# Retention and a squared-ReLU FFN: four heads in each half of x, a first stretch written out by hand

## The chip, the cores and the metric

The kernel runs on one core of one Trainium2 chip. The metric is the device time of one execution in microseconds (us); lower is better. The engines that matter are PE (TensorE, the matrix unit), DVE (VectorE), ACT (ScalarE), POOL (GpSimd) and SP (SyncE, which here only issues transfers). Each engine works through its own queue in order.

## The reference

The inputs q, k and v are float32 arrays of (8 batches, 8 heads, 576 positions, 64); w_in (512 x 2048) and w_out (2048 x 512) are float64 and are turned into float32 on the chip. Cut to what matters:

```python
scores = scale * np.matmul(q, k.transpose(0, 1, 3, 2))
gamma = 1.0 - 2.0 ** (-5.0 - np.arange(H))
Dmat = np.where(rel >= 0, gamma[:, None, None] ** rel, 0.0)   # rel = row - column
ret = scores * Dmat
attn = np.matmul(ret, v)
x = attn.transpose(0, 2, 1, 3).reshape(B * S, H * D)          # 4608 x 512
h = np.maximum(x @ w_in, 0.0)
out = h * h @ w_out
```

## The kernel before

**Two phases.** Phase one computes the retention (attn) chunk by chunk and feeds it into the first FFN product, g = relu(x @ w_in)², which goes to DRAM. Phase two (from about 565 us) reads g back and multiplies it by w_out. Both FFN products use a scheme with 7 products of sub-blocks in place of 8 (PRODUCTS), so sums of blocks are made by DVE; only the first block of 512 tokens is done plainly (`first_in`).

**Chunks.** The 576 positions of a batch are four chunks of 128 and one of 64; there are 40 chunks (`chunks`). A state matrix u (64 x 64 per head) carries what came before, so a chunk is two halves of 64 rows. For chunk i:

- `load(i)` transfers q, k and v from DRAM. q and k use three transfers each (L148 and L150, one half of the heads and then two groups of swapped heads), v one (L145).
- `scale_q(i)` multiplies q by its decay (L375: DVE for chunk 0, POOL for others); `scale_v(i)` does it for v (L468, POOL).
- `turn(i)` transposes k and q on PE into one PSUM tile of two banks (L422), one bank for each half of the rows. ACT copies all of k out of both banks (L425), DVE all of q (L426).
- `scores(i)` multiplies them on PE (L449), and DVE masks the result (L459 for chunks 0 to 3, L461 later).
- `retain_a` makes the second half's own products (L480) and adds the first half to u (L483); ACT copies u out (L489). `retain_b` multiplies q by u (L515). `retain_c` makes the first half's own products (L566) and adds the second half to u (L560). `x_out` lets ACT copy the result into xT (L543). The tiles x_ps and u_ps have one buffer each.

From chunk 11 on, DVE transposes by blocks (`flip`, L396), ACT moves the blocks (L411), and `whole` takes the place of the retain functions.

**Heads and halves of x.** xT holds x with its columns over 128 partitions and four groups. Before, group hp held the heads 2hp and 2hp+1 in its two halves of the partitions, as w_in lies in DRAM, so one transfer brought a piece of w_in. For hp of 2 and 3 the heads of q and k are swapped within a pair (`HEADS`, the third entry b is the half), so that the matmuls reach all four quarters of the array in turn; the two groups of swapped heads in `load` come from this.

**w_in.** It comes in 16 pieces of 512 KB (`fetch_w`, L196). Each piece is turned from 64-bit words into float32 in six parts (`round_parts`): one and two (L210, L214, DVE), beside (L218, L219, ACT), three, four and five (L222, L225, L228, DVE). `convert(n)` issues the next n parts. `fetch_raw(n)` issues the next n pieces, up to six ahead of the pieces that are done.

**The first block.** `first_in(j, halves)` multiplies piece j with xT (L671) for half of the 512 tokens (four matmuls of 256 columns) or all of them (512 columns), ACT applies Relu (L676), and DVE squares (L679). Half pieces 0 to 2 run as soon as the first 256 tokens are there.

**The order of the first stretch** is a loop with conditions on i (L856 to L898): for chunk i the retain functions of chunk i-1, then scores(i), scale_q(i+1) and turn(i+1), with convert and first_in between them and fills of idle matmuls (`warm`, L836 and L839).

**Pace.** After chunk 4, `ffn(i, half)` issues as many FFN steps as PACE asks for at the number of tokens that have gone by: pairs of (tokens, steps), with straight lines between. A block n of later FFN steps (`ffn_in`, L707) starts with four sums of x (`sum_x`, L633 to L636). They are issued one by one in the last steps of the block before, if block n's x is complete by then, and otherwise in a row at its start.

Of the kernel before, what the change touches and what calls it, by code (L numbers as in the profile page):

```python
# [40 lines left out]
def kernel(  # L41
# [90 lines left out]
    def load(i, names="qkv"):  # L132
# [4 lines left out]
        for name, pool, src in (("q", ld3, q), ("k", ld5, k), ("v", ld4, v)):  # L137
            if name not in names:
                continue
            t = got["qkv".index(name)] = pool.tile([128, H, D], F32, tag=name, name=f"{name}_ld")  # L140

            issue = nc.scalar if i == 0 and name != "q" else nc.sync
            at = src[b, :, c0:c0 + cs, :].rearrange("h s d -> s h d")
            if name == "v":
                issue.dma_start(t[:cs], at)  # L145
            else:

                issue.dma_start(t[:cs, 0:H // 2, :], at[:, 0:H // 2, :])  # L148
                for e in range(2):
                    issue.dma_start(t[:cs, H // 2 + e::2, :], at[:, H // 2 + 1 - e::2, :])  # L150
# [22 lines left out]

    def piece_src(j):
        wi, m, e = pieces[j]
        f = (m + e * N_M) * 128
        if wi == 0:
            return moe_w_in.rearrange("(c p) f -> p c f", p=128)[:, :, f:f + 128]
        return moe_w_out[f:f + 128, :].rearrange("p (c f) -> p c f", c=N_DM)

# [13 lines left out]
    def fetch_w(j):  # L194
        if j < len(pieces) and wide:
            nc.sync.dma_start(raw_of(j).bitcast(I64).rearrange("p (c f) -> p c f", c=N_DM), piece_src(j))  # L196
# [4 lines left out]
    def round_parts(j):  # L201
# [28 lines left out]
        if not wide:  # L230
            to = t if pieces[j][0] == 0 else t.rearrange("p o s f -> p (o s) f")
            return [lambda: nc.sync.dma_start(to, piece_src(j))] + [lambda: None] * 5
# [96 lines left out]
    load(1)  # L329
    fetch_raw(1)  # L330
    load(2)

# [22 lines left out]
    HEADS = [(hp, e, e if hp < HP // 2 else 1 - e) for hp in range(HP) for e in range(2)]  # L355

    def rows(half, n=64):
        return slice(64 * half, 64 * half + n)

# [52 lines left out]
    def turn(i):  # L414
# [10 lines left out]
        nc.scalar.copy(to[:, 1].rearrange("p d h t -> p h d t"), p[:, :n_h, 1, :, :])  # L425
        nc.vector.tensor_copy(to[:, 0].rearrange("p d h t -> p h d t"), p[:, :n_h, 0, :, :])  # L426
# [44 lines left out]
    def x_at(hp, b, h):  # L471
        return xp[0][rows(b), hp // 2, 0:256].rearrange("p (g t) -> p g t", g=2)[:, hp % 2, CH * h:CH * h + CH]

    def within(i, h):

        s = st[i]
        b_, ci, c0, cs = chunks[i]
        own, grow = [], []
        for hp, e, b in HEADS:
            own.append(lambda hp=hp, e=e, b=b: nc.tensor.matmul(  # L480
                x_at(hp, b, h), lhsT=s["vs"][rows(h), 2 * hp + b, :], rhs=s["ret"][rows(h), e, hp, :],
                start=clears(b, hp // 2), stop=False, skip_group_check=True))
            grow.append(lambda hp=hp, e=e, b=b: nc.tensor.matmul(  # L483
                u_ps[0][rows(e), hp, :], lhsT=loaded[i][1][rows(1 - h), 2 * hp + e, :], rhs=s["vs"][rows(1 - h), 2 * hp + b, :],
                start=(ci == 0 and h == 1 and hp == 0), stop=(hp == HP - 1), skip_group_check=True))
        return own, grow
# [4 lines left out]
    def retain_a(i):  # L491
# [4 lines left out]
        if ci == 0:  # L496
            u_ps[0] = ps_u.tile([128, HP, D], F32, tag="u", name="u_ps")
        if cs < C:
            return
        own, grow = within(i, 1)  # L500
        for j in range(0, len(own), 2):
            for f in own[j:j + 2] + grow[j:j + 2]:
                f()
        grown(i, 0)

    def retain_b(i):
# [3 lines left out]
        for h in reversed(range(cs // CH)):  # L510
# [3 lines left out]
            for hp, e, b in HEADS[0:2] + HEADS[4:6] + HEADS[2:4] + HEADS[6:8]:  # L514
                s["read"] = nc.tensor.matmul(  # L515
                    x_at(hp, b, h), lhsT=u[rows(e), hp, :], rhs=s["qT"][rows(e), hp, CH * h:CH * h + CH],
                    start=clears(b, hp // 2), stop=False, skip_group_check=True)
# [11 lines left out]
    def x_out(i, after):  # L529
# [5 lines left out]
        while at < tok + cs:  # L535
# [7 lines left out]
            nc.scalar.copy(xT[n][:, :, at - n * TOK:end - n * TOK].rearrange("p (a g) t -> p a g t", a=2),  # L543
# [10 lines left out]
    def grow_of(i, h):  # L554

        ci = chunks[i][1]
        if ci == 0 and h == 0:
# [3 lines left out]
            u[rows(e), hp, :], lhsT=loaded[i][1][rows(h), 2 * hp + e, :], rhs=st[i]["vs"][rows(h), 2 * hp + b, :],  # L561
            start=(ci == 0 and h == 0 and hp == 0), stop=(hp == HP - 1), skip_group_check=True) for hp, e, b in HEADS]

    def own_of(i, h, first):
        s = st[i]
        return [lambda hp=hp, e=e, b=b: nc.tensor.matmul(  # L566
            x_at(hp, b, h), lhsT=s["vs"][rows(h), 2 * hp + b, :], rhs=s["ret"][rows(h), e, hp, :],
            start=clears(b, hp // 2), stop=False, skip_group_check=True)
            for e in (first, 1 - first) for hp, e_, b in (HEADS[j] for j in (e, e + 4, e + 2, e + 6))]

# [10 lines left out]
    def whole(i):  # L581
# [16 lines left out]
        for h in range(cs // CH):  # L598
# [3 lines left out]
            for hp, e, b in HEADS[0:2] + HEADS[4:6] + HEADS[2:4] + HEADS[6:8]:  # L602
                m = nc.tensor.matmul(x_at(hp, b, h), lhsT=u[rows(e), hp, :], rhs=s["qT"][rows(e), hp, CH * h:CH * h + CH],
                                     start=clears(b, hp // 2), stop=False, skip_group_check=True)
# [168 lines left out]
    def step():  # L773
# [11 lines left out]
    PACE = ((4 * TOK + HALF // 4, N_0 + 2 * N_MP * NP - 2), (5 * TOK - HALF, N_0 + 3 * N_MP * NP - 2),  # L785
            (6 * TOK + HALF // 4, N_0 + 4 * N_MP * NP - 2), (8 * TOK + HALF // 4, N_0 + 6 * N_MP * NP - 2),
# [45 lines left out]
    def warm(count, wide):  # L832
        t = ps_f.tile([128, 512], F32, tag="f", name="idle_ps")
        for _ in range(count):
            if wide:
                nc.tensor.matmul(t[:, 0:128], lhsT=idle, rhs=idle, start=True, stop=True)  # L836
            else:
                for b in range(2):
                    nc.tensor.matmul(t[rows(b), 0:64], lhsT=idle[rows(0), rows(b)], rhs=idle[rows(0), 0:64], start=True, stop=True,  # L839
# [353 lines left out]
```

## Time and profile before

Five executions took 967.4 to 969.11 us, with a median of 967.99. The profiled execution:

| | |
|---|---|
| its own time | 969.06 us |
| span, from the first to the last instruction | 967.3 us |
| mean granted PE clock | 0.993 |
| copy of chunk 0's x, of chunk 1's (L543 starts) | 15.40 us, 24.69 us |
| copy of chunk 2's x, of chunk 3's (L543 starts) | 33.16 us, 38.68 us |
| first half piece of the FFN (L671) | 25.42 us |
| first piece over 512 tokens (L671, 512 columns) | 49.13 us |
| issues of q: of 128 KB, of 64 KB, of 32 KB | 32, 72, 16 (those of the short chunks among them) |
| v, 256 KB: median from issue to landing | 4.1 us |
| w_in piece, 512 KB: median from issue to landing | 5.8 us |

A row of the timeline has its start, its length, the engine, the line of the kernel, the operation, what it writes and reads, and in brackets how long the engine had been idle before it and what ended that. Times are from the start of the span. A matmul of float32 shows as two records.

### The profile page before, as it was taken

To read this page: it belongs to the slowest core of one execution; us is meant where nothing else is said; L and a number is where in the kernel's file an instruction comes from. 1 tells how busy PE (TensorE), PEld (TensorE's weight loads), DVE (VectorE), ACT (ScalarE), POOL (GpSimd) and SP (SyncE) were. 2 spreads that over 40 slices of the span, in tenths; PEclk is the share of its full clock that TensorE was granted. 3 is DMA by queue.
4 is the path that set the end of the run, shared out by engine and by line. 5 is a ranking of instruction groups with operands and counts; after the bars stand their busy time and mean duration, and the time that the engine had idled before them with its cause. 6 is when DMAs were issued, how large, how long until landed. Compare 5 with 4: busy or idle time off the path is not lost. (4 is left out here: it accounts for less than half of the span.)

```text
span 967.3 us, 24021 instructions
## 1 busy us (share of the span) xinstructions
PE 949.4 (98%) x10108; PEld 855.1 (88%) x10108; DVE 781.0 (81%) x1447; ACT 337.3 (35%) x808; POOL 129.8 (13%) x121
## 2 busy tenths in 40 slices
PE   6999999999999999999999999999999999999998
PEld 6755788888878888888888899999999999999998
DVE  3789799988897877988966597887888787887876
ACT  2544375865655866657621000000000000000000
POOL 3221223212213123222110000000000000000000
PEclk8999999999999999999999999999999999999999
DMA  9885657576649666684177966445354454524241
GB/s 204 224 226 152 184 164 198 172 248 201 192 133 289 185 159 198 201 244 143 61 293 292 357 247 255 155 157 186 123 194 163 160 197 162 203 99 174 88 175 44
DMA packets 172012, 181.43 MB, mean 188 GB/s; under 512 B 118144, under 2 KB 132480, under 8 KB 165248
## 3 DMA queue, kind: packets, MB, share of 16 engines
q1 hardware_dynamic: 169792, 179.38, 58.3%
q8 instruction: 79, 1.29, 0.6%
q10 hardware_dynamic: 2112, 0.52, 0.3%
q14 instruction: 29, 0.24, 0.1%
HBM read 109.36 MB, written 70.52 MB: 186 GB/s over the span
## 5 line engine op out<-in xcount | busy, mean ns | idle before, releaser
L707 PE MATMUL h_b<-room,w 128*128 128x256 f32 x768 | 183.4, 382 | 2.6 <-DVE room L634 1.9
L411 ACT COPY qk<-flip 32x256 f32<-32x256 f32 x416 | 167.4, 402 | 8.4 <-DVE flip L396 2.3
L707 PEld LDWEIGHTS h_b<-room,w 128*128 128x128 f32 x768 | 144.3, 190 | 24.1 <-issue 2.2
L1042 PE MATMUL o_b<-w,room 128*128 128x128 f32 x1168 | 144.4, 275 | 0.2 <-DVE room L994 0.2
L1042 PEld LDWEIGHTS o_b<-w,room 128*128 128x128 f32 x1168 | 137.2, 192 | 0.4 <-DVE room L994 0.4
L1042 PE MATMUL o_c<-w,room 128*128 128x128 f32 x1008 | 123.0, 275 | 0.0
L707 PE MATMUL h_a<-room,w 128*128 128x256 f32 x512 | 122.0, 381 | 0.0
L707 PE MATMUL h_c<-room,w 128*128 128x256 f32 x512 | 121.8, 381 | 0.0
L1042 PEld LDWEIGHTS o_c<-w,room 128*128 128x128 f32 x1008 | 117.7, 192 | 0.0
L707 PEld LDWEIGHTS h_a<-room,w 128*128 128x128 f32 x512 | 96.5, 190 | 14.1 <-issue 0.5
L1056 ACT COPY r<-o_a 128x128 f32<-128x128 f32 x53 | 14.1, 266 | 271.6 <-PE o_a L1042 230.9
L707 PEld LDWEIGHTS h_c<-room,w 128*128 128x128 f32 x512 | 96.6, 190 | 13.4
L1042 PE MATMUL o_a<-w,a 128*128 128x128 f32 x688 | 85.7, 275 | 0.0
L724 POOL TENSOR_TENSOR room<-room 128x512 f32<-128x512 f32 x32 | 35.8, 1119 | 342.1 <-ACT room L723 331.7
L1042 PEld LDWEIGHTS o_a<-w,a 128*128 128x128 f32 x688 | 81.2, 192 | 0.1
L714 DVE SCALAR_TENSOR_TENSOR room<-room 128x512 f32<-128x512 f32 x96 | 71.8, 748 | 3.3
L671 PE MATMUL h_ps<-room,w 128*128 128x512 f32 (+1 forms) x152 | 60.3, 545 | 1.1 <-ACT room L543 0.7
L375 POOL TENSOR_TENSOR q_ld<-q_ld,dv 128x512 f32<-128x512 f32 (+1 forms) x39 | 44.3, 1135 | 81.9 <-DMA q_ld<-in_q_dram 74.1
L468 POOL TENSOR_TENSOR v_ld<-v_ld,dv 128x512 f32<-128x512 f32 (+1 forms) x40 | 50.7, 1269 | 11.9 <-DMA v_ld<-in_v_dram 7.0
L726 DVE TENSOR_TENSOR room<-h_b,room 128x512 f32<-128x512 f32 x32 | 22.0, 689 | 37.3 <-PE h_b L707 37.3
L671 PEld LDWEIGHTS h_ps<-room,w 128*128 128x128 f32 x152 | 28.6, 196 | 24.2 <-issue 20.6
L566 PE MATMUL x_ps<-qk,v_ld 64*64 64x64 f32 x1024 | 49.6, 224 | 0.0
(109 smaller groups left out, 1381.4 us busy)
## 6 DMA issues: line engine op xcount, KB each, us to landing
g_dram<-room SPq DMA_DIRECT2D x32, 1280.0 KB, 5.7
a<-g_dram SPq DMA_DIRECT2D x30, 1024.0 KB, 6.0
room<-g_dram SPq DMA_DIRECT2D x15, 1024.0 KB, 5.7
w<-w_dram SPq DMA_DIRECT2D x7, 1792.0 KB, 9.7
out_dram<-room SPq DMA_DIRECT2D x17, 512.0 KB, 3.3
w<-in_moe_w_in_dram SPq DMA_DIRECT2D x16, 512.0 KB, 5.8
w<-in_moe_w_out_dram SPq DMA_DIRECT2D x16, 512.0 KB, 4.4
v_ld<-in_v_dram SPq DMA_DIRECT2D x31, 256.0 KB, 4.1
```

The costliest lines, as they stand in the source:

```text
L375: engine.tensor_tensor(t, t, dv[:cs, :, NCH + ci:NCH + ci + 1].to_broadcast([cs, H, D]), op=ALU.mult)
L411: nc.scalar.copy(*moves.pop(0)[2:])
L468: nc.gpsimd.tensor_tensor(vs[:cs], vs[:cs], dv[:cs, :, ci:ci + 1].to_broadcast([cs, H, D]), op=ALU.mult)
L566: return [lambda hp=hp, e=e, b=b: nc.tensor.matmul(x_at(hp, b, h), lhsT=s["vs"][rows(h), 2 * hp + b, :], rhs=s["ret"][rows(h), e, hp, :], ...
L671: nc.tensor.matmul(p.rearrange("p h t -> p (h t)"), lhsT=w[:, c, :], rhs=xT[0][:, c, lo * HT:hi * HT], start=(c == 0), stop=(c == N_DM - 1))
L707: nc.tensor.matmul(p[:, mm, :], lhsT=w[:, c, :], rhs=xs[n][right][:, c, :], start=(j in OPENS and mm == 0 and c == 0), stop=(j in CLOSES a ...
L714: nc.vector.scalar_tensor_tensor(t, t, 0.0, t, op0=ALU.max, op1=ALU.mult)
L724: nc.gpsimd.tensor_tensor(g["A11"], g["A11"], g["A11"], op=ALU.mult)
L726: nc.vector.tensor_tensor(g["A22"], p, p15, op=ALU.add)
L1042: nc.tensor.matmul(p, lhsT=s["lefts"][left][:, m, :], rhs=w_out[j][:, m, WO_SLOT[right], :], start=(i in OPENS and m == 0), stop=(i in CLO ...
L1056: nc.scalar.copy(r[:, 0, 0:128], p)
```

## The change

A half of the partitions of x now holds four heads: heads 0 to 3 in the lower, 4 to 7 in the upper (`HEADS`: b is hp // 2, and the bank of x_ps is e). q, k and the decays keep the natural order of the heads, so q and k are one transfer each. A w_in piece is now two transfers, one for each half of the partitions (`in_parts`). In `turn`, for chunks of 128, ACT copies the first bank (k and q of the first 64 rows) and DVE the second. The first stretch is written out as a list. It holds scores(1) ahead of retain_b(0), fewer idle matmuls (one pair of 512 columns in place of 28 pairs of 64), w_in pieces fetched earlier, and 29 parts of conversion by its end where there were 32. One point of PACE is gone. `within` is gone, and `retain_a` uses `own_of` and `grow_of`.

```diff
@@ load
-            at = src[b, :, c0:c0 + cs, :].rearrange("h s d -> s h d")
-            if name == "v":
-                issue.dma_start(t[:cs], at)
-            else:
-                issue.dma_start(t[:cs, 0:H // 2, :], at[:, 0:H // 2, :])
-                for e in range(2):
-                    issue.dma_start(t[:cs, H // 2 + e::2, :], at[:, H // 2 + 1 - e::2, :])
+            issue.dma_start(t[:cs], src[b, :, c0:c0 + cs, :].rearrange("h s d -> s h d"))
@@ pieces of w_in
+    def in_parts(j):
+        wi, m, e = pieces[j]
+        f = (m + e * N_M) * 128
+        for half in range(2):
+            of = slice(half * d_model // 2, (half + 1) * d_model // 2)
+            yield rows(half), moe_w_in[of, f:f + 128].rearrange("(c p) f -> p c f", p=D)
...
     def fetch_w(j):
-        if j < len(pieces) and wide:
-            nc.sync.dma_start(raw_of(j).bitcast(I64).rearrange("p (c f) -> p c f", c=N_DM), piece_src(j))
+        if j >= len(pieces) or not wide:
+            return
+        to = raw_of(j).bitcast(I64)
+        if pieces[j][0]:
+            nc.sync.dma_start(to.rearrange("p (c f) -> p c f", c=N_DM), piece_src(j))
+        else:
+            for at, part in in_parts(j):
+                nc.sync.dma_start(to[at].rearrange("p (c f) -> p c f", c=N_DM), part)
@@ start
     load(0)
-    load(1)
+    load(1, "qk")
     fetch_raw(1)
+    load(1, "v")
     load(2)
+    fetch_raw(2)
@@ heads
-    HEADS = [(hp, e, e if hp < HP // 2 else 1 - e) for hp in range(HP) for e in range(2)]
+    HEADS = [(hp, e, hp // (HP // 2)) for hp in range(HP) for e in range(2)]
...
-    def x_at(hp, b, h):
-        return xp[0][rows(b), hp // 2, 0:256].rearrange("p (g t) -> p g t", g=2)[:, hp % 2, CH * h:CH * h + CH]
+    def x_at(hp, e, b, h):
+        return xp[0][rows(b), e, 0:256].rearrange("p (g t) -> p g t", g=2)[:, hp % 2, CH * h:CH * h + CH]
@@ turn
-        nc.scalar.copy(to[:, 1].rearrange("p d h t -> p h d t"), p[:, :n_h, 1, :, :])
-        nc.vector.tensor_copy(to[:, 0].rearrange("p d h t -> p h d t"), p[:, :n_h, 0, :, :])
+        if n_h == 2:
+            nc.scalar.copy(to[:, :, :, 0, :], p[:, 0, :, :, :])
+            nc.vector.tensor_copy(to[:, :, :, 1, :], p[:, 1, :, :, :])
+        else:
+            nc.scalar.copy(to[:, 1].rearrange("p d h t -> p h d t"), p[:, :n_h, 1, :, :])
+            nc.vector.tensor_copy(to[:, 0].rearrange("p d h t -> p h d t"), p[:, :n_h, 0, :, :])
@@ retain_a
-        own, grow = within(i, 1)
-        for j in range(0, len(own), 2):
-            for f in own[j:j + 2] + grow[j:j + 2]:
-                f()
+        beside_each(own_of(i, 1, 1), grow_of(i, 0), range(0, H, 2))
         grown(i, 0)
@@ x_out
-            nc.scalar.copy(xT[n][...].rearrange("p (a g) t -> p a g t", a=2),
+            nc.scalar.copy(xT[n][...].rearrange("p (g a) t -> p a g t", a=2),
                            p[:, :, :, at - tok:end - tok])
@@ pace
-    PACE = ((4 * TOK + HALF // 4, N_0 + 2 * N_MP * NP - 2), (5 * TOK - HALF, N_0 + 3 * N_MP * NP - 2),
-            (6 * TOK + HALF // 4, N_0 + 4 * N_MP * NP - 2), (8 * TOK + HALF // 4, N_0 + 6 * N_MP * NP - 2),
+    PACE = ((4 * TOK + HALF // 4, N_0 + 2 * N_MP * NP - 2), (6 * TOK + HALF // 4, N_0 + 4 * N_MP * NP - 2), (8 * TOK + HALF // 4, N_0 + 6 * N_MP * NP - 2),
             (9 * TOK, N_0 + 7 * N_MP * NP - 2))
@@ warm
-                    nc.tensor.matmul(t[rows(b), 0:64], lhsT=idle[rows(0), rows(b)], rhs=idle[rows(0), 0:64], start=True, stop=True,
-                                     skip_group_check=True)
+                    nc.tensor.matmul(t[rows(b), :], lhsT=idle[rows(0), rows(b)], rhs=idle[rows(0), 0:1].to_broadcast([64, 512]),
+                                     start=True, stop=True, skip_group_check=True)
@@ the first stretch: the part of the loop for i <= N_EARLY goes, and this comes (two calls to a line here)
     turn(0)
+    load(3); scores(0)
+    scale_q(1, nc.gpsimd); warm(1, False)
+    turn(1); fetch_raw(1)
+    retain_a(0); convert(3)
+    scores(1); scale_q(2, nc.gpsimd)
+    retain_b(0); retain_c(0)
+    load(4); fetch_raw(2)
+    convert(2); retain_a(1)
+    turn(2); convert(1)
+    retain_b(1); retain_c(1)
+    load(5); fetch_raw(1)
+    convert(3); first_in(0, (0,))
+    convert(1); scores(2)
+    scale_q(3, nc.gpsimd); retain_a(2)
+    convert(2); turn(3)
+    first_in(1, (0,)); convert(3)
+    retain_b(2); retain_c(2)
+    load(6); fetch_raw(1)
+    convert(1); scores(3)
+    convert(2); scale_q(4, nc.gpsimd)
+    first_in(2, (0,)); convert(3)
+    retain_a(3); turn(4)
+    retain_b(3); retain_c(3)
+    load(7); fetch_raw(2)
+    step(); scores(4)
+    convert(3); scale_q(5, nc.gpsimd)
+    step(); convert(5)
+    for i in range(N_EARLY + 1, N_CH + 1):
...
@@ decays
-    order = [h if h < H // 2 else h ^ 1 for h in range(H)]
-    by_s = (gamma[order, None, None] ** s / math.sqrt(D)).transpose(2, 0, 1)
+    by_s = (gamma[:, None, None] ** s / math.sqrt(D)).transpose(2, 0, 1)
```

The other calls of x_at, `own_of` and `grow_of` follow the new indices (the bank e, and head 2hp + e in place of 2hp + b).

## The prediction

> **What bounds the kernel now.** I read the page first: span and share of each engine, then the 40 slices.
>
> ```profile
> span 967.3 us, 24021 instructions
> PE 949.4 (98%) x10108; PEld 855.1 (88%) x10108; DVE 781.0 (81%) x1447; ACT 337.3 (35%) x808; POOL 129.8 (13%) x121
> ...
> PE   6999999999999999999999999999999999999998
> ...
> DVE  3789799988897877988966597887888787887876
> ...
> PEclk8999999999999999999999999999999999999999
> DMA  9885657576649666684177966445354454524241
> ```
>
> PE is busy 98% of the span. Only the first slice (24 us) is poor, so a change can pay only by letting PE reach its full stream sooner, or by removing a hole later. The busy times by stretch show where:
>
> ```profile
> 10.00:20.00 10.00, 8.92 (x277) 8.14 (x274) 4.03 (x10) 4.08 (x8) 3.18 (x3) 0.77 1.01 252
> 20.00:30.00 10.00, 7.78 (x156) 6.66 (x155) 5.79 (x10) 2.97 (x6) 4.22 (x4) 0.66 0.59 134
> 30.00:40.00 10.00, 8.88 (x223) 7.45 (x220) 9.62 (x17) 6.00 (x14) 2.33 (x3) 1.00 0.81 196
> 285.00:290.00 5.00, 3.13 (x15) 2.47 (x14) 4.93 (x9) 3.32 (x8) 0.00 (x0) 1.00 0.01 3
> ```
>
> The columns are PE, PEld, DVE, ACT, POOL, granted clock, DMA share, GB/s. From 10 to 20 us the transfers are full (1.01) and the clock is low (0.77); from 285 to 290 us PE works 3.13 of 5. Then the timeline of PE, for what ends each gap:
>
> ```profile
> 8.42 1.13 PE L449 MATMUL sc_ps<-qk 64*64 64x64 f32 x32 [1.41 <-DVE qk L426]
> ...
> 22.22 0.80 PE L515 MATMUL x_ps<-qk,u_sb 64*64 64x64 f32 x18 [2.83 <-issue]
> ...
> 25.42 3.34 PE L671 MATMUL h_ps<-room,w 128*128 128x256 f32 x8
> ...
> 29.96 1.99 PE L671 MATMUL h_ps<-room,w 128*128 128x256 f32 x8
> ...
> 48.04 0.69 PE L449 MATMUL sc_ps<-qk 64*64 64x64 f32 x32 [1.24 <-DVE qk L426]
> 49.13 6.28 PE L671 MATMUL h_ps<-room,w 128*128 128x512 f32 x14
> ...
> 287.57 1.97 PE L707 MATMUL h_b<-room,w 128*128 128x256 f32 x8 [1.87 <-DVE room L634]
> ```
>
> The same half piece takes 3.34 us at 25.42 and 1.99 at 29.96: the clock. From 49.13 on PE runs full pieces, and the list of waits has nothing over 0.7 us on PE after that but the 1.87 at 287.57. The chain of waits goes back only to 565 us and is all PE there, so the second phase is not touched. **So I compare two times: when the first full-width piece (j=3) starts, and the hole at 287.** What PE gains there lasts to the end if DVE keeps up: in the timeline the last conversion step (L228) of pieces 5 to 15 ends 5.0 to 7.1 us before PE starts that piece.
>
> **The change, part by part.**
>
> *One transfer for q and k.* Each chunk issues 3 transfers where there were 7, 160 fewer in all. On SP an issue takes 0.46 to 0.6 us. Bytes and 256-byte runs stay, and SP sets nothing after 60 us, so later this is worth 0: PE hides it, with q scaled a chunk ahead of its use. At the start it counts: q0's last issue ended at 2.73, now it ends near 1.75. q0 came at 5.80 (DVE's scaling starts there). Between 0 (the bytes decide) and 1.0 earlier I take 0.7, as the last landing follows its issue by 3 us.
>
> *Two transfers per w_in piece.* 16 issues more, 0.6 us each on SP, 9.6 us over 100 us in which SP also drops about 48 issues: 0. The Trainium skill, page "DMA: Bandwidth & Descriptors", section "Rules for kernel authors", speaks against this: two transfers to halves of the partitions share the same engines, one over 128 partitions is better. By that rule it is 0.6 us of issue per piece for nothing, and on the path at most once, for piece 0. The split is needed here only because a half of x now holds four whole heads.
>
> *Copies by banks.* ACT's copy of k ran 7.06 to 7.65, DVE's of q from 7.68 to 8.37, one after the other on the same two banks. By banks both start at 7.06 and the longer ends at 7.75: 0.62 gained for chunk 0. For chunks 1 to 3 it lies in the chain below; from chunk 5 on PE has pieces to do meanwhile: 0.
>
> *The new order.* Scores of the first chunk start at 8.42 - 0.7 - 0.62 = 7.1. Then PE's queue as it will stand, with rows of before (low clock until 14 us, as then): scores(0) 1.13, to 8.2; the one wide idle pair, four records of 512 columns (0.43 apart at full clock, so 0.9 if side by side and up to 3.4 at half clock in a row; I take 1.7, twice the lower), to 9.9; turn(1) 1.12, 11.0; retain_a(0) 1.13, 12.1; scores(1) 1.13, 13.2; retain_b and c(0) 1.45, 14.7; the x copy and u copy 0.86, 15.5 (x_ps and u_ps have one buffer); retain_a(1) 0.7, turn(2) 0.7, retain_b and c(1) 1.46: the x of chunk 1 starts at **18.5**, before it was 24.69. The transfers allow it: by the landings of before (q1 8.15, v1 10.26, q2 13.97, v2 17.0, less 0.7), piece 0 is there at about 10.5, piece 1 at 18, q3 at 21.
>
> *Code.* Of the 24.69, 2.83 us are the wait named issue at 22.22, 0.45 another at 15.91. The page shows an instruction queue (q8, 79 packets, 1.29 MB: 16 KB each, and 1.29 MB over 20216 PE records is 64 B, so 256 records or 128 matmuls a packet). The two waits are 142 matmuls and 6.3 us apart. I read them as code that comes late while transfers are full. The change drops 104 of the 112 idle records of L839. At the new places matmul 77 is in turn(1) at 10.8, 219 at the end of retain_a(1) at 16.3, 361 in retain_a(2) after 23: 5.5 us where 6.3 were needed, then enough. So 0.8 (bounds 0 and 2.8): x of chunk 1 at 19.3.
>
> *From there to the full pieces* the order puts DVE behind PE and ACT. Each step waits for the one before: x copy 0.59, first_in(0) 1.99, scores(2) 0.65, mask 0.76, parts four and five of piece 1 1.4, first_in(1) 1.99, its Relu and the two ACT parts of piece 2 1.7, part three 0.69, mask(3) 0.76, four and five 1.4, first_in(2) 1.99, Relu and ACT parts 1.7, u copy 0.38, retain_b and c(3) 1.46: 17.5, so the x of chunk 3 at 36.8; it was 38.68. Of a lead of 5.4 only 1.9 is left: piece 2's and 3's ACT parts stand behind a Relu that waits for PE, and DVE is idle behind them. Then x copy 0.59, first_in(0) 2.0, scores(4) 0.4, mask 0.7, DVE's three to five of piece 3 2.07 (they are queued behind that mask now), a square and four shorter parts 1.9, copy 0.69, scores(5) and retain_c(4) 1.3: 9.6. Piece 3 starts at 46.4 instead of 49.13: **2.7 us gained** (0.7 with the whole code wait, 3.5 with none).
>
> Three DVE parts (2.07 us) come later than before in the count of parts by then (29, not 32). They come out of the slack of 5.0, so 0; without it PE would wait up to 2.
>
> *PACE.* The dropped point asked for 98 steps at token 2496, two short of block 4, just ahead of the chunk that completes block 4's x. So L634's sums were made in a row at the block's start. On the straight line from 70 (2064) to 126 (3088), 2496 asks for 93.6: the last steps of block 3 come after that x, and the sums go in one by one as at the other blocks. **1.87 gained**; bounds 2.24 (PEld's gap) and 0.
>
> *Head order.* x's bank now follows e. Record counts stay. Reads now alternate as scores do (x32 in 0.65 against 0.69 for reads): 0.
>
> **Sum.** 2.7 + 1.87 = 4.6. The profiled execution took 969.06 (span 967.3 and 1.76 around it): 964.5. It is 1.07 above the median 967.99, so on the median 963.4.
>
> **The clock.** The clock rose to 1.00 by 30 us with 112 small idle records, most of which go. PE's gaps in my chain stay below 2 us where before one of 2.83 stood ahead of the slow piece, so I keep the clock of before up to 14 us and full from there. The Trainium skill, "TensorE: Matmul & The Clock Gate", "Part 1: The HAM clock gate", says that the throttled state is the default and some 3.4 us of activity lift it; by it, thinner warming could hold the half clock for one window more, 1.35 on a half piece.
>
> **Rivals.**
> 1. *A longer lead*: the chain from 19.3 is less strict than I wrote it and most of the 6.2 us lasts. For: DVE works only 5.79 of 10 us from 20 to 30. Against: its order is fixed. 967.99 - 6.2 - 1.87 = 959.9.
> 2. *The start gives nothing*: code, late transfers (1.5 MB more of w_in stand ahead of chunk 5's q) or DVE take it back, and only the hole at 287 goes: 966.1.
> 3. *Slower, by the clock*: with 104 idle records gone the gate falls back at the first gap and PE runs at half rate up to the full pieces. Six half pieces at +1.35, of which one was already paid, 6.75; chunks 2 and 3 at +2.1 (scores 1.13 for 0.65, turn 1.12 for 0.71, retain in proportion): 4.2. Together 11, and 11 - 4.6 = 6.4 slower, or 2.2 if only the pieces are on the path: 970 to 974, 971 taken. It decides if the clock from 20 to 40 us is under 0.7. For: 0.66 from 20 to 30 before. Against: real work fills that stretch now.
> 4. *The copies don't run side by side*, if DVE is still busy when a bank is ready: 0.6 per chunk at most, inside the range of the forecast.
>
> **Chances.** Forecast (with rival 4) 0.57; longer lead 0.14; only the hole 0.17; slower 0.12. A measurement of this kernel tells 0.2% (1.9 us) from no change. The forecast's own range is 962 to 965.5, so it and the longer lead are faster; the third lies on the edge at 966.1, a third of it faster: 0.57 + 0.14 + 0.05 = 0.76, same 0.13, slower 0.11. The range takes in the longer lead and the third case: 959.5 to 968.3.
>
> **What would show it.** In the changed profile: scores(0) near 7.1, the two copies of a turn at the same time; the x of chunk 1 near 19 and of chunk 3 near 37; the first 128x512 piece near 46.4; no wait of h_b on L634; issue waits of PE under 1 us; clock 1.00 from 20 us. A first full piece later than 49, or holes on L707 behind conversion steps, would make me wrong; one before 43 means that I made the chain too strict.

## The result and the profile after

The changed kernel takes 969.74 us (median of 21 runs, 967.82 to 973.06), the kernel before on the same chips 967.65 (40 runs). The ratio is 1.0021, with a 95% interval of 1.0013 to 1.0029: slower by 0.2%, where 963.4, faster by 0.5%, was forecast.

The profiled execution took 973.06 us, 3.3 above the median and the slowest of the 21. Most of this excess is not at its start: from ACT's copy of x at 357.31 us to the end it needs 613.99 us, where the same stretch takes 611.6 in the profiles of e3, e4 and e17 below. First its page: the span, the slices of the span, and the queue that carries the transfers.

```profile
span 971.3 us, 23541 instructions
...
PE   7899999999999999999999999999999999999998
...
DVE  4499789988889887987976597888888788787876
...
PEclk9699999999999999999999999999999999999999
DMA  9997576686857876766168966545354454524241
...
q1 hardware_dynamic: 167520, 179.37, 61.4%
```

PE's first slice is better than before (7 for 6), the second slice now has the low clock (6). The queue is busy for 61.4% of the time, before for 58.3%, with as many bytes. Then the same stretches as before and one more; the columns are PE, PEld, DVE, ACT, POOL, granted clock, DMA share, GB/s.

```profile
10.00:20.00 10.00, 8.74 (x244) 6.74 (x240) 5.63 (x11) 4.44 (x9) 3.17 (x3) 1.00 1.24 219
20.00:30.00 10.00, 8.22 (x119) 6.19 (x123) 6.99 (x12) 3.60 (x9) 2.65 (x3) 0.83 1.11 189
30.00:40.00 10.00, 7.20 (x138) 5.67 (x132) 3.87 (x8) 3.63 (x8) 3.13 (x3) 0.67 1.13 209
40.00:50.00 10.00, 9.33 (x114) 7.34 (x114) 4.07 (x6) 2.00 (x5) 2.11 (x2) 0.65 1.13 197
285.00:290.00 5.00, 5.00 (x104) 4.28 (x103) 4.97 (x6) 1.28 (x4) 3.31 (x3) 1.00 0.23 91
```

The hole at 287 is gone: PE is busy for all 5 us. The clock column has 1.00 up to 20 us and then 0.83, 0.67 and 0.65. The 1.00 of the first 16 us can't be right; these rows of PE show it:

```profile
11.23 0.69 PE L430 MATMUL t_ps<-w,k_ld 64*128 64x64 f32 x8
...
17.71 0.47 PE L430 MATMUL t_ps<-w,k_ld 64*128 64x64 f32 x8
```

The same eight records take 0.69 us at 11.23 and 0.47 at 17.71. Before they took 0.69 at 10.76, where the column has 0.50, and 0.46 at 17.11, where it has 1.00. So PE ran at the low rate up to about 16 us, as before and some 2 us longer; the column missed it. From 21 us on the times of the half pieces agree with the column. The DMA share is higher than before (1.24 against 1.01 from 10 to 20 us) for fewer bytes (219 GB/s against 252). DVE works 3.87 of 10 us from 30 to 40, where it worked 9.62: it waits. What it waits for shows in the timelines of PE, DVE and ACT, taken together here around the second and third half piece.

```profile
20.52 1.97 PE L664 MATMUL h_ps<-room,w 128*128 128x256 f32 x8 [0.92 <-ACT u_sb L487]
26.13 3.35 PE L664 MATMUL h_ps<-room,w 128*128 128x256 f32 x8 [0.18 <-DVE w L238]
...
34.16 3.75 PE L664 MATMUL h_ps<-room,w 128*128 128x256 f32 x8 [2.80 <-DVE w L238]
...
55.23 4.99 PE L664 MATMUL h_ps<-room,w 128*128 128x512 f32 x11
```
```profile
31.12 0.69 DVE L232 SCALAR_TENSOR_TENSOR w<-w,w 128x512 f32<-128x512 uint32 x1 [2.14 <-ACT w L229]
...
40.46 0.42 DVE L438 COPY qk<-t_ps 128x256 f32<-128x256 f32 x1 [5.44 <-ACT qk L437]
```
```profile
29.52 0.38 ACT L669 ACTIVATE room<-h_ps 128x256 f32<-128x256 f32 x1 [2.94 <-PE h_ps L664]
29.80 0.71 ACT L228 ACTIVATE w<-w,exp_bias 128x512 uint32<-128x512 uint32 x1
30.41 0.68 ACT L229 ACTIVATE w<-w 128x512 f32<-128x512 uint32 x1
```

Read from the bottom up: ACT idles 2.94 us until PE has finished the half piece of 26.13, takes its Relu (L669), and only then makes its two parts of piece 2. DVE idles 2.14 us for these parts, and PE waits 2.80 us for DVE. It is a ring: each engine waits for the one before, and at half clock the PE part of it is 3.35 us where at full clock it is 1.97. The first full-width piece starts at 55.23, 6.1 later than before. From there to the end it is 971.3 - 55.23 = 916.1, where it was 967.3 - 49.13 = 918.2: 2.1 gained, although this run loses 2.7 against before behind 357.31. So the loss that a usual run has lies in the first 55 us.

### The profile page after: what moved, and what is told of

Same layout as the page of the kernel before. It is cut to its first block, busy times and chain, and to the rows that moved or that the text cites. A ratio compares the mean times of both kernels' runs of the same rounds, so it can differ in the third digit from the quotient of the medians.

```text
span 971.3 us, 23541 instructions
## 1 busy us (share of the span) xinstructions
PE 952.3 (98%) x10000; PEld 854.7 (88%) x10000; DVE 784.6 (81%) x1447; ACT 337.5 (35%) x808; POOL 133.4 (14%) x121
## 3 DMA queue, kind: packets, MB, share of 16 engines
q1 hardware_dynamic: 167520, 179.37, 61.4%
## 4 chain that ended last, share of the span: by engine, by line
PE 90%; DVE 4%; DMA 2%; SPq 2%; issue 1%; ACT 0%; POOL 0%; DVEq 0%; POOLq 0%
PE o_b L1042 17%; PE h_b L700 16%; PE o_a L1042 11%; PE o_c L1042 11%; PE h_a L700 11%; PE h_c L700 10%; PE h_ps L664 6%; PE x_ps L559 3%; PE sc_ps L461 2%; DMA g<-g_dram 1%; PE u_ps L553 1%; PE x_ps L596 1%; SPq L143 1%; DMA q_ld<-in_q_dram 1%; SPq L206 1%
## 5 line engine op out<-in xcount | busy, mean ns | idle before, releaser
L700 PEld LDWEIGHTS h_c<-room,w 128*128 128x128 f32 x512 | 96.7, 190 | 13.3
L664 PE MATMUL h_ps<-room,w 128*128 128x512 f32 (+1 forms) x152 | 63.9, 573 | 4.6 <-DVE w L238 3.0
L559 PEld LDWEIGHTS x_ps<-qk,v_ld 64*64 64x64 f32 x1152 | 45.4, 139 | 15.7 <-issue 14.9
L559 PE MATMUL x_ps<-qk,v_ld 64*64 64x64 f32 x1152 | 56.5, 228 | 1.7 <-DVE qk L471 1.0
L383 POOL TENSOR_TENSOR q_ld<-q_ld,dv 128x512 f32<-128x512 f32 (+1 forms) x39 | 46.3, 1186 | 81.3 <-DMA q_ld<-in_q_dram 77.2
L664 PEld LDWEIGHTS h_ps<-room,w 128*128 128x128 f32 x152 | 30.6, 209 | 28.4 <-issue 23.3
```

The lines of the kernel that those rows point to most:

```text
L383: engine.tensor_tensor(t, t, dv[:cs, :, NCH + ci:NCH + ci + 1].to_broadcast([cs, H, D]), op=ALU.mult)
L559: return [lambda hp=hp, e=e, b=b: nc.tensor.matmul(x_at(hp, e, b, h), lhsT=s["vs"][rows(h), 2 * hp + e, :], rhs=s["ret"][rows(h), e, hp, : ...
L664: nc.tensor.matmul(p.rearrange("p h t -> p (h t)"), lhsT=w[:, c, :], rhs=xT[0][:, c, lo * HT:hi * HT], start=(c == 0), stop=(c == N_DM - 1))
L700: nc.tensor.matmul(p[:, mm, :], lhsT=w[:, c, :], rhs=xs[n][right][:, c, :], start=(j in OPENS and mm == 0 and c == 0), stop=(j in CLOSES a ...
```

## The experiments

All times are medians in us. The kernel before took 967.2 to 967.9 beside them, and the ratio stands against it. "Before" and "after" are the two kernels.

| run | kernel | median | lowest to highest | ratio, 95% interval |
|---|---|---|---|---|
| e1 | before, PACE point out | 964.02 | 963.38 to 966.05 | 0.9957 (0.9941 to 0.9974) |
| e2 | before, w_in by halves of the partitions | 974.83 | 974.0 to 975.74 | 1.0067 (1.0052 to 1.0081) |
| e5 | before, w_in by columns | 968.04 | 965.65 to 971.96 | 1.0005 (0.9992 to 1.0018) |
| e11 | e1, one transfer each for q and k | 963.36 | 963.1 to 965.25 | 0.9959 (0.9946 to 0.9972) |
| e3 | after, old order of the first stretch | 967.51 | 966.79 to 967.99 | 0.9995 (0.9987 to 1.0004) |
| e4 | after, five more pairs of idle matmuls | 968.29 | 966.28 to 969.16 | 0.9999 (0.9988 to 1.001) |
| e7 | after, one transfer per w_in piece | 970.32 | 967.92 to 972.81 | 1.0025 (1.0014 to 1.0036) |
| e8 | after, t_ps as two tiles | 968.76 | 966.74 to 969.84 | 1.0009 (1.0 to 1.0018) |
| e6 | e1 in the new order | 966.92 | 964.25 to 974.03 | 0.9998 (0.9978 to 1.0018) |
| e9 | e6, more idle matmuls | 965.99 | 963.26 to 972.18 | 0.9993 (0.9973 to 1.0013) |
| e10 | e6, conversion parts ahead | 965.94 | 961.96 to 968.48 | 0.9977 (0.9963 to 0.9992) |
| e12 | e6, both | 961.54 | 961.02 to 962.52 | 0.9938 (0.9924 to 0.9951) |
| e15 | e12, t_ps as two tiles | 960.81 | 960.21 to 961.8 | 0.993 (0.9917 to 0.9943) |
| e13 | after, both | 962.73 | 961.44 to 966.93 | 0.9958 (0.9943 to 0.9972) |
| e14 | e13, one transfer per w_in piece | 966.21 | 960.77 to 969.96 | 0.9981 (0.9963 to 1.0) |
| e16 | e13, t_ps as two tiles | 962.8 | 961.84 to 967.79 | 0.9955 (0.9939 to 0.9972) |
| e17 | e13 again | 962.76 | two runs | 0.9948 (0.993 to 0.9965) |

### e1: the PACE point alone

```diff
-    PACE = ((4 * TOK + HALF // 4, N_0 + 2 * N_MP * NP - 2), (5 * TOK - HALF, N_0 + 3 * N_MP * NP - 2),
+    PACE = ((4 * TOK + HALF // 4, N_0 + 2 * N_MP * NP - 2),
```

> The kernel before with one point of PACE taken out, nothing else. Theory pace (the sums of block 4 are made in a row because the point calls two steps too many ahead of that block's x): the wait of h_b on L634 at 287 us is gone, the time is 1.9 us below before, near 965.8. Rival (the wait moves to another block or the PE stream was not the bound there): within 0.5 us of before.

It gave 3.4 to 3.6, about twice the expected. ACT's copies of x are milestones that both kernels have. Two of them in the timeline of before, then the same two in that of e1:

```profile
228.23 0.35 ACT L543 COPY room<-x_ps 128x256 f32<-128x256 f32 x1
...
356.02 0.59 ACT L543 COPY room<-x_ps 128x512 f32<-128x512 f32 x1 [0.99 <-PE x_ps L566]
```
```profile
226.54 0.35 ACT L543 COPY room<-x_ps 128x256 f32<-128x256 f32 x1
...
350.60 0.58 ACT L543 COPY room<-x_ps 128x512 f32<-128x512 f32 x1 [0.99 <-PE x_ps L566]
```

Between them before needs 127.79 us and e1 124.06: 3.73 less. Two more stretches of before show what went beside the 1.87 at 287:

```profile
260.00:270.00 10.00, 9.49 (x147) 8.43 (x137) 6.53 (x11) 6.80 (x16) 1.04 (x1) 1.00 0.62 157
...
310.00:320.00 10.00, 9.34 (x115) 8.00 (x114) 8.39 (x13) 8.62 (x21) 3.52 (x3) 1.00 0.83 190
```

PE lacks 0.51 and 0.66 us there; in e1 both stretches are full. 1.87 + 0.51 + 0.66 = 3.04. Over the whole stretch between the two copies PE is idle for 3.30 us before and for 0.48 in e1. The remaining 0.9 is busy time (124.49 and 123.58); why it is less is not shown.

### e2 and e5: two transfers per w_in piece, by halves of the partitions and by columns

The edits, for the pieces of w_in (those of w_out stay):

```diff
-            nc.sync.dma_start(raw_of(j).bitcast(I64).rearrange("p (c f) -> p c f", c=N_DM), piece_src(j))
+            to = raw_of(j).bitcast(I64).rearrange("p (c f) -> p c f", c=N_DM)
@@ e2
+                for at in (slice(0, 64), slice(64, 128)):
+                    nc.sync.dma_start(to[at], piece_src(j)[at])
@@ e5
+                for c in (0, N_DM // 2):
+                    nc.sync.dma_start(to[:, c:c + N_DM // 2], piece_src(j)[:, c:c + N_DM // 2])
```

> The kernel before with each w_in piece as two transfers of 64 partitions, nothing else. Theory transfers (a transfer into half of the partitions is slower, so all that stands behind it in the queue lands later): q of chunks 2 and 3 is scaled 1 to 3 us later than the 13.97 and 22.12 us of before, GB/s stay below 225 where before had 262 to 266 between 8 and 20 us, time 1 to 3 us above before. Theory clock or order: landings as before, time within 0.5 us of before.

> The kernel before with each w_in piece as two transfers again, but each to all 128 partitions (two of the four columns of rows each). Theory (transfers into half of the partitions move less per us, their number costs nothing): within 1.5 of the kernel before, 966.5 to 969, about 240 GB/s as the mean of the four 4 us windows from 4 to 20 us. Rival (two transfers in place of one cost as much however they are cut): 973 to 976 as with the halves, about 220 GB/s.

By halves the kernel before loses 7.2 to 7.4, more than the 1 to 3 expected; by columns, with as many transfers, nothing. So the number of transfers is free and the halves are not. The stretch from 4 to 20 us of e2, then of e5, and one line of e2's DVE timeline:

```profile
4.00:20.00 16.00, 12.87 (x334) 11.69 (x334) 5.25 (x11) 4.82 (x10) 5.29 (x5) 1.00 1.18 219
```
```profile
4.00:20.00 16.00, 12.68 (x334) 11.51 (x334) 6.14 (x11) 4.71 (x10) 5.30 (x5) 1.00 1.05 245
```
```profile
48.69 0.43 DVE L215 TENSOR_SCALAR w<-w 128x512 uint32<-128x512 uint32 x1 [3.77 <-DMA w<-in_moe_w_in_dram]
```

With the halves the queues are busier (1.18 against 1.05) and move less (219 against 245 GB/s). DVE then waits 3.77 us for piece 5, and scores(5), whose copy of q is queued behind that part on DVE, waits with it; before, the same wait was 0.91. The first full piece comes at 54.07, 4.9 later than before, and at the low clock (0.50 from 52 to 56 us). The Trainium skill says in "SBUF — State Buffer", section "Door 1: The DMA port swizzle", that the rate of a transfer goes by how many of the 16 ports to SBUF its partitions reach, and that one half of the partitions reaches 8; its table has about 218 GB/s as the limit there, half of its 436. The measured 219 lies at this figure. That the ports set it is not shown: q, k and v go to 128 partitions in the same stretch, and with w_in to 128 as well the windows of 4 us reach 267 (e5) and 274 (e6), not 436.

### e3, e4, e7 and e8: parts of the changed kernel undone or mended

e3 puts the first loads, the loop for `i <= N_EARLY` and the small idle matmuls of the kernel before into the changed one.

> The changed kernel with the first stretch in the order of before (its loop, its first loads, its 28 pairs of small idle matmuls); new transfers, head order, copies by banks and PACE stay. Theory order or clock (the new order of the first stretch loses what it gains): first 512-column piece near 49 us, time near before less the 1.9 of PACE, 965.8. Theory transfers: the first piece comes 2 us or more after 49, time near 968 or above.

e4 adds these pairs of idle matmuls:

```diff
     retain_c(1)
+    warm(1, False)
...
     scores(2)
+    warm(1, False)
...
     scores(3)
+    warm(3, False)
```

> The changed kernel with idle matmuls of 512 columns added at three places of the first stretch where PE waits (one pair after retain_c(1), one after scores(2), three after scores(3)). Theory clock (the first stretch loses its lead because PE runs at half clock from 27 to 46 us): the granted clock stays at 1.00 there, the first 512-column piece comes 4 to 6 us ahead of the 55.2 of the changed kernel, the median falls 2 to 5 us below 969.7. Rival order (DVE and ACT in turn bind, PE's rate does not matter): the clock rises and the time stays within 1 us of 969.7, or rises by the up to 2 us of the added matmuls.

> The changed kernel with one transfer of 128 partitions for each w_in piece, the rows of w_in as in the kernel before, so that x meets other rows of w_in and the output is another one; the work is the same. Theory (the halves cost most of what is lost): 969.7 less 5 to 7, 962.5 to 965, first 512-column piece at 47 to 50. Rival (order and clock lose it): 968 or more, piece at 53 or later.

```diff
-            for at, part in in_parts(j):
-                nc.sync.dma_start(to[at].rearrange("p (c f) -> p c f", c=N_DM), part)
+            f = (pieces[j][1] + pieces[j][2] * N_M) * 128
+            nc.sync.dma_start(to.rearrange("p (c f) -> p c f", c=N_DM),
+                              moe_w_in.rearrange("(c p) f -> p c f", p=128)[:, :, f:f + 128])
```

> The changed kernel with the two banks of t_ps as two tiles for the first four chunks, so that the copy on VectorE waits for TensorE and not for ScalarE's copy. Theory (the copies ran in a row only because both banks were one tile): both copies of a turn start within 0.1 us, scores(0) at 7.15 to 7.25 in place of 7.76, x of chunk 1 at 18.5 to 19.3; the whole moves by 0 to -1.0 us since late transfers and clock decide later. Rival (two engines reading PSUM at the same time hold each other up): the two copies start together but one takes 1.1 us or more, scores(0) stays at 7.6 or later.

The edit of e8, cut to the two tiles (they are rearranged as the one tile was, and each copy reads its own):

```diff
-        p = ps_t.tile([128, 2, 512], F32, tag="t", name="t_ps")
+        p0 = ps_t.tile([128, 2, 512], F32, tag="t", name="t_ps")
+        p1 = ps_f.tile([128, 512], F32, tag="f", name="t1_ps") if n_h == 2 and i < N_EARLY else p0[:, 1]
```

The old order in the changed kernel is 2.2 better than the new one (e3), so the new order loses. But it does not reach the 965.8 of that theory: 3.5 are left against e1, which has the old order too. More idle matmuls alone hold the clock at 1.00 from 20 to 48 us, with half pieces of 1.97 to 1.99, and give 1.5 (e4), less than the 2 to 5 expected. In e4's profile the first full piece comes at 51.22, 4.0 earlier than in the changed kernel; but from 48 to 52 us PE is busy for only 2.13 of 4, the clock is 0.62 from 52 to 56, and by ACT's copy of x at 230.97 it has lost 1.7 of the 4.0 again. One transfer per piece gives nothing (e7): the rival's number, against my theory. I had taken e2's 7.4 for the loss of the changed kernel too, and that fell. The issues of w_in on SP may say why: in e2 the pieces 3, 4 and 5 are issued at 28.7, 34.6 and after 41.9; in the changed kernel at 22.1, 26.2 and 27.8. The new order fetches them so much earlier that the lower rate would be hidden; this is a reading of the issues, and no run changes them alone.

e8 shows why the two copies of a turn stayed in a row. In the changed kernel, ACT's and DVE's timelines:

```profile
7.12 0.59 ACT L434 COPY qk<-t_ps 128x512 f32<-128x512 f32 x1 [3.91 <-PE t_ps L430]
```
```profile
7.74 0.69 DVE L435 COPY qk<-t_ps 128x512 f32<-128x512 f32 x1 [1.41 <-ACT qk L434]
```

And in e8:

```profile
7.29 0.59 ACT L436 COPY qk<-t_ps 128x512 f32<-128x512 f32 x1 [4.08 <-PE t_ps L432]
```
```profile
7.33 0.69 DVE L437 COPY qk<-t_ps 128x512 f32<-128x512 f32 x1 [0.81 <-PE t_ps L432]
```

They read different banks, but both banks were one tile, and the program made DVE wait for ACT's semaphore. As two tiles the copies start 0.04 us apart and neither is longer. The time moved by 1.0 (969.74 to 968.76), and the intervals overlap.

### e6, e9, e10 and e12: the new order on the transfers of before

e6 puts the change's first loads, order and idle matmuls into e1; its transfers, copies and head order stay those of before.

> The kernel before, its transfers as they were, with the new order of the first chunks, the new idle matmuls and no PACE point at token 2496. The kernel before without that PACE point took 964.0. Theory (the new order does bring the lead, and the half-partition transfers ate it): the first 512-column piece starts at 46 to 48.5 and the time is 961.5 to 963.8. Rival (the order itself loses, by the half clock between 24 and 48 us and by conversion steps queued behind a mask): first 512-column piece at 50 or later, 965 to 968.

> The kernel before with the new order and no PACE point (966.9 in an earlier run), and five more pairs of 512-column idle matmuls where PE waits: one pair after the x of chunk 1, one after scores(2), three after scores(3). Theory (the new order loses to the old one, 966.9 against 964.0, by the half clock): clock 1.00 in every 4 us window from 20 to 48 us, third half piece in 1.99 us, 964 to 965.3. Rival (the conversion steps behind ScalarE's Relu lose it, whatever the clock): 966 to 967.5, the third half piece still starts at 32 or later.

> The same new order, without more idle matmuls, but the first three parts of pieces 2 and 3 are issued ahead of the half piece that stood before them, so that ScalarE makes its two parts before it waits for that piece's Relu, and parts three to five of piece 3 ahead of the mask of chunk 4. Theory (the strict chain through the Relu loses 3.5 us at the third half piece): it starts 1.5 to 3 us earlier than 32.95, first 512-column piece at 46.5 to 48.5, 963 to 965. Rival (the clock decides, the chain only moves the wait): 966 to 967.5.

> The new order with both: the conversion parts ahead and the five more pairs of idle matmuls. Theory (chain and clock each cost their part): 962 to 964, below the 964.0 of the kernel before without the PACE point if the lead of 5 us at the x of chunk 1 lasts. Rival (late transfers of q, k and w_in hold the start at 47 us or later whatever the order): 964 to 966.

```diff
     turn(3)
+    convert(3)
     first_in(1, (0,))
-    convert(3)
...
+    convert(3)
     first_in(2, (0,))
-    convert(3)
...
     step()
-    scores(4)
     convert(3)
+    scores(4)
```

The edit of e10 stands above, that of e9 is e4's, e12 has both. The order alone costs 2.9 over e1 (966.92 against 964.02): the rival's number, and the first full piece of its profile comes at 49.69. Either mending alone gives about 1 in the median, with intervals that overlap that of e6, and does not reach its theory's range; both together give 5.4. My reading is that they are two halves of one loss: a wait in the ring brings the half clock, and the half clock makes the ring longer. e12 is 2.5 better than e1, so the lead is real once both are done. The timeline of e12, ACT first, then PE:

```profile
26.68 0.72 ACT L218 ACTIVATE w<-w,exp_bias 128x512 uint32<-128x512 uint32 x1 [1.09 <-DVE w L210]
27.30 0.66 ACT L219 ACTIVATE w<-w 128x512 f32<-128x512 uint32 x1
27.86 0.37 ACT L678 ACTIVATE room<-h_ps 128x256 f32<-128x256 f32 x1
```
```profile
31.93 1.99 PE L673 MATMUL h_ps<-room,w 128*128 128x256 f32 x8
...
45.48 0.70 PE L673 MATMUL h_ps<-room,w 128*128 128x512 f32 x1
```

ACT's two parts now come before the Relu (L678), the third half piece has no wait ahead of it and runs in 1.99 us, and the first full piece starts at 45.48. The medians of e9 and e10 hide how far their runs spread. e10's profiled run, its fastest (961.96), is within the range of e12 without the added idle matmuls. PE there:

```profile
32.66 1.97 PE L673 MATMUL h_ps<-room,w 128*128 128x256 f32 x8 [2.51 <-DVE w L228]
```

The wait is 2.51 us, and the clock stays at 1.00 from 20 to 60 us all the same. Four of e10's twelve runs lie at 962.0 to 963.0, the others at 964.7 to 968.5; the five of e12 lie at 961.0 to 962.5. So the conversion parts ahead give all of it in some runs, and with the idle matmuls all five runs have it. What makes the slower runs of e10 slow is not shown.

### e11: one transfer each for q and k

The edit is that of `load` in the change, on e1.

> The kernel before without the PACE point (964.0) and with one transfer each for q and k of a chunk in place of three; the heads of the last two pairs then stand in the other order in q and k, so the output is another one, the work is the same. Theory (fewer issues are worth 0 to 0.7 us at the start and nothing later): 963.2 to 964.3, q of chunk 0 scaled 0 to 0.7 earlier than 5.80. Rival (as one transfer q and k get a smaller part of the rate beside the 512 KB pieces of w_in and come later): scaling of q2 and q3 1 us or more later than at 13.97 and 22.12, 965.5 to 968.

963.36 against 964.02: the theory holds, the number of transfers is free here too.

### e13 to e17: the changed kernel mended

> The changed kernel itself with both edits that brought the new order to 961.5 on the transfers of the kernel before: conversion parts ahead of the half piece, five more pairs of idle matmuls. Theory A (the half-partition transfers cost in the changed kernel what they cost in the kernel before): 965.5 to 969, about 220 GB/s from 4 to 20 us. Theory B (in the changed kernel the chain through the Relu and the half clock lose all, and the transfers are hidden): 961 to 963.5.

> The same with one transfer of 128 partitions for each w_in piece, the rows of w_in as in the kernel before, so that x meets other rows of w_in and the output is another one. Theory A: 961 to 962.5, 3 to 7 less than the run with the halves. Theory B: within 1 of it. If it is 964 or more, something else of the change (one transfer each for q and k, copies by banks, head order) costs beside the new order.

> The new order with both edits on the transfers and the head order of the kernel before (961.5), and the two copies of a turn by banks, each bank a tile of its own, for the first four chunks. Theory (each copy pair in a row costs 0.6 of the chain at the start): both copies start within 0.1 us, 960 to 961.3. Rival (the start is set by late transfers and by the conversion steps): 961.3 to 962.5.

> The changed kernel with the conversion parts ahead, the five more pairs of idle matmuls and the two banks as two tiles: all that helped, on the layout and the transfers of the change. The same on the layout of the kernel before took 960.8. Theory (q and k in one transfer, head order and half-partition transfers cost nothing once the order hides them): 960.5 to 962. Rival (the late landings of the halves still cost): 962.5 to 965.

> The changed kernel with the parts ahead and the idle matmuls once more, for a profile: its 12 runs fell into two groups, 7 at 961.4 to 963.0 and 5 at 965.5 to 966.9, and the profile was of the second, with a wait named issue of 2.5 us at 39.2 and the half clock behind it. Theory (the wait makes the group): a profiled run under 963 has no issue wait over 1 us from 30 to 45 us and the clock at 1.00 there; one over 965 has both. Rival: the groups come from the landings, and a run under 963 has the wait too.

The two edits of e12 on the changed kernel give 7.0 (969.74 to 962.73, theory B); 1.2 is left against e12. One transfer per piece (e14) did not make the median better; three of its runs lie at 960.8 to 961.8, as fast as e12, the other nine at 965.5 to 970.0, and why is open. e15, on the transfers of before, is the fastest of all, 960.81; its 0.7 over e12 is within what the two ranges overlap. e16 is not better than e13, so on the layout of the change the two tiles bring nothing that can be told.

The times of e13 fall into two groups, seven at 961.4 to 963.0 and five at 965.5 to 966.9, none between; the median of the faster group is 961.8, near e12's 961.54. The profile of e13 is of the second group (966.91), that of e17 of the first (962.78). PE in e13, and its windows there; then the windows of e17:

```profile
39.16 0.26 PE L553 MATMUL u_ps<-v_ld,k_ld 64*64 64x64 f32 x1 [2.48 <-issue]
...
40.75 3.78 PE L664 MATMUL h_ps<-room,w 128*128 128x256 f32 x8 [0.67 <-ACT room L536]
```
```profile
36.00:40.00 4.00, 1.52 (x64) 1.28 (x63) 3.48 (x5) 0.35 (x1) 1.34 (x1) 0.86 0.91 203
40.00:44.00 4.00, 3.33 (x12) 2.50 (x8) 0.00 (x0) 0.86 (x2) 1.59 (x2) 0.50 1.27 210
```
```profile
36.00:40.00 4.00, 3.33 (x105) 2.95 (x94) 2.51 (x4) 1.77 (x5) 1.06 (x1) 1.00 0.96 206
40.00:44.00 4.00, 4.00 (x45) 2.99 (x44) 3.29 (x8) 0.96 (x3) 1.06 (x1) 1.00 1.01 156
```

The same program, once with a wait named issue of 2.48 us and once without. With it PE is busy for 1.52 of 4 us, the clock falls to 0.50, the next half piece takes 3.78 for 1.99, and the run is 4.1 longer. The profiled run of e16 (966.14) has the wait too, 2.41 at 39.28. In these three profiles the wait goes with the longer time. That the wait is code that comes late is my reading, not shown. The Trainium skill says in "Runtime: NRT & Kernel Launch", section "Instruction fetch mechanics", that the sequencer streams its code in 16 KiB blocks and that crossing into the next one is mostly hidden; if this wait is that crossing, it was not hidden here.

## Why the prediction was wrong

**The step that failed is the stretch from the x of chunk 1 to the first full piece, added up at full clock**: "so I keep the clock of before up to 14 us and full from there". The sum was 17.5 + 9.6 = 27.1 us. The profiled run took 55.23 - 19.63 = 35.6: 22.3 to the x of chunk 3 (41.97) and 13.3 from there.

By a comparison with e4, the larger part in that run is the clock. PE ran at full rate from about 17 to 26 us, where the second half piece took 3.35 us. After the wait of 2.80 in front of the third one (PE is busy for 1.84 of 4 us from 32 to 36) it stayed at half rate up to about 47: 3.75 and 3.78 for half pieces that take 1.97 to 1.99 at full rate. With more idle matmuls (e4) all half pieces run at full rate, and the same stretch takes 51.22 - 21.19 = 30.0. Rival 3 had named this, with "under 0.7" from 20 to 40 us as its condition; it was 0.83 and 0.67, and the kernel became slower by 2 us, the lower end of the 2.2 to 6.4 there. I gave it 0.12.

The rest is the ring. What the prediction said of it, "piece 2's and 3's ACT parts stand behind a Relu that waits for PE, and DVE is idle behind them", is what the profile shows, 2.14 and 5.44 us of it: the chain had the right form and no room in it. With the parts ahead and the clock held, e12 took 36.39 - 19.29 = 17.1 to the x of chunk 3 and 9.1 from there, and its first full piece came at 45.48, where 46.4 had been predicted. On the changed kernel the two edits bring 962.7 (e13), where 963.4 was forecast; holding the clock alone brings 1.5 of these 7.0.

**The x of chunk 1** came at 19.63 (19.3 predicted), but by terms that offset each other. q0's scaling came 0.16 earlier (5.80 to 5.64), not 0.7. The copies did not run side by side (rival 4, though not for its reason: DVE was free and waited for ACT's copy), and scores(0) started at 7.76, not 7.1. The code wait of 0.8 at that place did not show in this run. That the number came out is luck.

**Two w_in transfers at 0** agrees with e7 in the new order, but the reason that I gave, cheap issues, is not enough: on the kernel before the same split costs 7.4, most of it in the wait of 3.77 us and what it drags behind it. There one transfer over 128 partitions, which I set aside, is better; two transfers by columns cost nothing (e5). In the new order the pieces are issued up to 14 us earlier, which would hide it.

**PACE** was right in its mechanism and mis-sized: 3.7 for 1.87, outside of my bounds, since I counted only the one wait that the list named and not the two stretches in which PE also lacked half a microsecond or more, nor the busy time. In the changed kernel it gave as much: the two copies of x are 357.31 - 233.29 = 124.0 us apart.

**Three DVE parts later at 0** held: after 60 us PE waits for no conversion step in the changed kernel's profile.

In medians: 967.65, less 3.6 (PACE, e1), plus 2.9 (new order, e6), leaves 2.8 up to the 969.74 of the changed kernel for the halves, the single transfers, the copies and the head order. It isn't settled which of them has it: e7 takes the halves out and gains nothing, e11 shows the single transfers free, in the old order the four together cost 3.5 (e3 against e1), and with ring and clock mended only 1.2 is left (e13 against e12).

## What to carry to other kernels

Before an order written out by hand is costed, follow each wait around: where ACT's work for the next piece stands behind the Relu of this one, PE, ACT and DVE wait for each other in a ring. Here the two edits against it (prepare first, consume after; hold the clock with idle matmuls where a wait stays) were worth 1 to 1.5 us one by one in the medians and 5 to 7 us together. A gap of some 2.5 us in a thin stretch can cost more than itself: in e13 the half clock followed it, in e10 it did not. Check a clock column against the time of equal rows. And the wait that a list names can be half of what its cause costs: sum PE's missing time over the whole stretch.

## What was not expected of the hardware

With w_in in transfers to 64 partitions the core moved 218 to 223 GB/s from 4 to 20 us in all eight profiles that have them, with w_in in transfers to 128 partitions 242 to 250 in all eleven others; between e2 and e5, which differ in nothing else, it is 219 at a DMA share of 1.18 against 245 at 1.05. Two copies out of PSUM by ACT and DVE, from two banks, ran at the same time at 0.59 and 0.69 us, as long as one after the other. One program (e13, e17) has two groups of times 4 us apart; in the profiles the slower one has a wait of 2.48 us on PE and a clock that falls after it. And the granted clock of a profile can miss a low rate: e13 has 0.52 from 8 to 12 us and e17 1.00, while the eight records of turn(1)'s k take 0.69 us in both.
